# Four held first-layer tiles in two PSUM banks instead of three in three

## The chip, the cores and the metric

The kernel runs on one core of one Trainium2 chip. The metric is the time of one execution on the device in microseconds (us); a kernel is judged by the median of its runs. Beside the timed runs one execution was taken by the hardware profiler; all rows below are from it. Engines are PE (matmuls), PEld (its weight loads), ACT, DVE and POOL; SP issues the DMA loads and stores.

## The reference

Three layers follow each other, all in fp32. 1152 tokens (2 batches of 576) have width 512, in attention 8 heads of 64.

```python
# 1. attention: a coarse part on means of 4 positions, and a local part
a = softmax(scale * q_d @ k_d.T) @ v_d            # repeated 4 times along the sequence
l = softmax(where(abs(i - j) < 4, scale * q @ k.T, -1e9)) @ v
x = repeat(a, 4) + l                              # 1152 x 512
# 2. a feed-forward layer
h = x @ w_in                                      # 512 -> 2048
x = (h / (1 + exp(-h))) @ w_out                   # 2048 -> 512
# 3. four experts, each weighted by p
y = sum(p[:, e:e+1] * (relu(x @ w1[e]) @ w2[e]))  # 512 -> 1024 -> 512
```

## The kernel before

Each fp32 product is made of three matmuls on rounded operands (high x high, high x low, low x high), so an operand is kept as a high part (`xh`, `gh`) and a low part (`xl`, `gl`). Tokens are worked on in chunks of 256, 320, 256 and 320 columns.

**Attention** is cut into 16 jobs (batch, half of the sequence, pair of heads), numbered 0 to 15; jobs 0 to 3 give the four 128-row slices (`hp`) of x for chunk 0, jobs 4 to 7 those for chunk 1, and so on. Of a job: scores on PE (L328, L334), maximum and subtraction on DVE (L341, L342), exponentials on ACT (L346, L368), the coarse scores (L352), sums and normalisation on DVE (L349, L366 to L377), transposes on PE (L388, L390) that ACT evacuates (L391 to L398), products with the values (L416, L420), and the split into `xh` (ACT, L432) and `xl` (DVE, L433).

**The feed-forward layer** takes its weights in units of 2048 columns; units 0 and 1 are for the first layer of the first half (8 tiles of 128 features), units 2 and 3 for its second layer, unit 4 is the first of the second half. Each unit is loaded in four quarters of 512 KB (L164) into one of three staging tiles. A quarter is rebuilt from a packed form: two passes on ACT (L189, L190), two on DVE (L191, L195; the second frees the staging tile, and with it the next load), then ACT rounds the high part (L197) and POOL subtracts to get the low part (L198). The first layer of a tile (`g1_step`) is 12 matmuls into a PSUM bank of the pool `mm`, which has three; its evacuation (`g1_evac`) is a tanh on ACT (L514), a product on DVE (L515), and one step later the split into `gh` (L520) and `gl` (L521). The second layer (`g2_step`) adds up 24 matmuls per tile over the 8 feature tiles.

**The hold.** While attention for chunk 0 runs, the first tiles of its first layer are already summed up, slice by slice as the jobs deliver it (`start_mm`, one call per `hp`). They stay in their banks until the main loop reaches them and only evacuates them.

**The order.** Every step has a priority (`prio`, ticks in `at_tick`); a scheduler lays the instructions of each engine into a fixed list from these and from its own estimate of the durations, so a different hold changes the lists of all engines as far as they are not tied. On the chip each engine works its list strictly in order, SP too: an instruction that waits holds up all behind it.

Of the kernel before, what the change touches and what calls it, by code (L numbers as in the profile page):

```python
# [21 lines left out]
HP = NH // 2  # L22
# [18 lines left out]

SPLIT_AT = (-14, -11, -8, -6, -4, -4, -4, -4, -1, -1)
LOAD_AT = (-27, -13, -10)
HOLD = 3
LEAD_LOAD = 23
LEAD_SPLIT = 8
LEAD_ATTN = 11
# [14 lines left out]
def attention_moe_kernel(ctx, tc, kqa, kqb, qtl, va, vb, w64, w1d, w2d, dpr, out):  # L62
    nc = tc.nc
    PE, ACT, DVE, POOL, SP = nc.tensor, nc.scalar, nc.vector, nc.gpsimd, nc.sync
# [57 lines left out]
    def follow(i, earlier, reason):  # L122
        tc.add_manual_dep(i.ins, earlier.ins.name, mybir.DependencyInfo(mybir.DependencyClass.NoSync, mybir.DependencyReason.DATA),
                          reason=reason)
# [192 lines left out]
    def after(i, earlier):  # L317
        follow(i, earlier, "PSUM bank")
# [174 lines left out]
    def mm3(ps, pairs, first, last):  # L493
        n = len(pairs)
        ins = [PE.matmul(out=ps, lhsT=l, rhs=r, start=(first and i == 0), stop=(last and i == n - 1))  # L495
               for i, (l, r) in enumerate(pairs)]
        return ins[0], ins[-1]

    def g1_pairs(u0, ft, k, c):
        wh, wl = unit[u0 + ft // 4]  # L500
        s = slice(k * 512 + (ft % 4) * 128, k * 512 + (ft % 4) * 128 + 128)
        return [(wh[:, s], xh[:, k, c]), (wh[:, s], xl[:, k, c]), (wl[:, s], xh[:, k, c])]
# [8 lines left out]
    def g1_evac(ps, ft, n):  # L511
        th = tmp_p[0].tile([128, tmp_p[1]], F32, tag="th", name="th")
        gf = tmp_p[0].tile([128, tmp_p[1]], F32, tag="gf", name="gf")
        ACT.activation(out=th[:, 0:n], in_=ps[:, 0:n], func=ACTF.Tanh, scale=0.5)  # L514
        DVE.scalar_tensor_tensor(out=gf[:, 0:n], in0=th[:, 0:n], scalar=1.0, in1=ps[:, 0:n],  # L515
                                 op0=ALU.add, op1=ALU.mult)
        flush()

        def fin():
            latest[ACT] = ACT.activation(out=gh[ft][:, 0:n], in_=gf[:, 0:n], func=ACTF.Copy)  # L520
            latest[DVE] = DVE.tensor_tensor(out=gl[ft][:, 0:n], in0=gf[:, 0:n], in1=gh[ft][:, 0:n].bitcast(F32), op=ALU.subtract)  # L521

        pend.append(fin)

    def mm_tile():
        return mm_p.tile([128, 512], F32, tag="mm", name="mm")
# [239 lines left out]
    hold = []  # L766

    def start_mm(hp):
        for i in range(HOLD):
            if hp == 0:  # L770
                hold.append(mm_tile())
            mm3(hold[i][:, 0:256], g1_pairs(0, i, hp, slice(0, 256)), hp == 0, hp == HP - 1)

    main_parts.append(start_mm)
    plan_jobs()
    for hp in range(HP):
        at_tick(FIRST + PER * hp + 8, 9, start_mm, hp)
# [31 lines left out]
    def next_step(n=1):  # L809
        prio(step[0])  # L810
        step[0] += n

    for hf in range(2):
        u0 = 4 * hf
        dt = 48 / (12 * len(CHUNKS[hf]))
        for ci, (o, n) in enumerate(CHUNKS[hf]):
            lastc = ci == len(CHUNKS[hf]) - 1
            for ft in range(8):
                next_step(dt)
                if hf == 0 and ci == 0 and ft < HOLD:  # L820
                    g1_evac(hold[ft], ft, 256)
# [138 lines left out]
```

## Time and profile before

| | |
|---|---|
| median of 3 runs | 691.39 us |
| lowest and highest | 689.97 and 691.98 us |
| span of the profiled execution, first to last instruction | 693.6 us |
| mean granted TensorE clock in it | 0.974 |
| PE / DVE / ACT / POOL busy | 659.5 / 440.3 / 332.0 / 247.5 us |

Of the profiled execution only the span is given, no time of its own. A row of the timeline reads: start in us, duration in us, engine, line, operation, tile written <- tiles read, number of instructions, and in brackets the idle time of the engine just before and what ended it. Durations of matmuls contain their way through the array, so that neighbours overlap.

### The profile page before, as it was taken

Reading aid. Unit: us, or ns where it says so; the run is one execution under the profiler, and the core shown is the slowest. Engines: PE = TensorE matmul, PEld = TensorE weight load, DVE = VectorE, ACT = ScalarE, POOL = GpSimd, SP = SyncE. Lnnn points to the kernel's source line nnn. Section 1 sums busy time; section 2 is a strip of 40 time slices with the busy share of each in tenths; the row PEclk is TensorE's granted clock in tenths of the full one; section 3 lists DMA queues with packets and bytes.
Section 4 is the critical chain, followed back from the end, with each engine's and each line's share of the span. In section 5 each row is a group of like instructions: output and inputs, shape, how many; then the busy total and the mean of one; then the engine's idle time right before and its main releaser. Section 6 shows DMA issues by size and latency. Waiting matters only on the chain.

```text
span 693.6 us, 13797 instructions
## 1 busy us (share of the span) xinstructions
PE 659.5 (95%) x5516; PEld 641.9 (93%) x5516; DVE 440.3 (63%) x882; ACT 332.0 (48%) x753; POOL 247.5 (36%) x346
## 2 busy tenths in 40 slices
PE   4779779999999999999999999999999999999996
PEld 3659669999999999999999999999999999999996
DVE  4678967638664643675665985548855669756444
ACT  4559766647653532544335643345533356433321
POOL 4344762114240000344264432456232654322210
PEclk9597989999999999999999999999999999999999
DMA  8665663105250210042001420004300010000001
GB/s 248 215 183 166 184 176 96 34 1 161 92 174 1 81 44 1 1 144 70 1 1 48 136 61 1 1 2 122 93 31 1 1 60 3 1 32 17 17 31 45
DMA packets 16927, 48.16 MB, mean 69 GB/s; under 512 B 2976, under 2 KB 4256, under 8 KB 16864
## 3 DMA queue, kind: packets, MB, share of 16 engines
q1 hardware_dynamic: 16864, 47.29, 22.0%
q8 instruction: 43, 0.70, 0.4%
q14 instruction: 20, 0.16, 0.1%
HBM read 44.93 MB, written 2.36 MB: 68 GB/s over the span
## 4 chain that ended last, share of the span: by engine, by line
PE 83%; DMA 6%; DVE 6%; ACT 2%; issue 2%; POOL 1%; SPq 0%; ACTq 0%; DVEq 0%; POOLq 0%
PE mm L495 53%; PE p L699 26%; DMA stg<-in_w_dram 3%; DMA vg<-in_va_dram 2%; DVE dec L191 1%; DVE dec L195 1%; DVE gl L521 1%; PE s L328 1%; PE o L420 1%; PE t L388 1%; PE o L416 1%; DVE acc L727 1%; DVE gf L515 0%; POOL vg L265 0%; PE s L352 0%
## 5 line engine op out<-in xcount | busy, mean ns | idle before, releaser
L495 PE MATMUL mm<-xh,wbuf 128*128 128x256 f32 (+2 forms) x1280 | 268.7, 296 | 3.4 <-ACT xh L432 2.6
L495 PEld LDWEIGHTS mm<-xh,wbuf 128*128 128x128 f32 x1280 | 211.0, 190 | 4.7 <-ACT xh L432 3.0
L495 PE MATMUL mm<-xl,wbuf 128*128 128x256 f32 (+2 forms) x640 | 189.8, 297 | 0.0
L681 POOL TENSOR_TENSOR r<-r 128x128 f32<-128x128 f32 x160 | 93.5, 597 | 183.2 <-ACT r L675 143.7
L684 DVE TENSOR_TENSOR h<-r,h 128x384 fp32r<-128x384 f32 (+1 forms) x128 | 91.4, 717 | 64.6 <-ACT h L683 64.4
L495 PEld LDWEIGHTS mm<-xl,wbuf 128*128 128x128 f32 x640 | 121.6, 190 | 0.1
L683 ACT ACTIVATE h<-r 128x384 fp32r<-128x384 f32 (+1 forms) x128 | 73.2, 577 | 85.3 <-POOL r L681 54.1
L495 PE MATMUL mm<-gh,wbuf 128*128 128x256 f32 (+2 forms) x512 | 106.0, 300 | 6.4 <-ACT wbuf L197 3.5
L699 PE MATMUL p<-wext,h 128*128 128x256 f32 x672 | 91.5, 279 | 0.0
L495 PEld LDWEIGHTS mm<-gh,wbuf 128*128 128x128 f32 x512 | 83.8, 191 | 8.0 <-ACT wbuf L197 3.7
L699 PE MATMUL p<-wbuf,h 128*128 128x256 f32 x672 | 84.5, 278 | 0.0
L699 PEld LDWEIGHTS p<-wext,h 128*128 128x128 f32 x672 | 84.4, 188 | 0.0
L699 PEld LDWEIGHTS p<-wbuf,h 128*128 128x128 f32 x672 | 81.2, 188 | 0.0
L495 PE MATMUL mm<-gl,wbuf 128*128 128x256 f32 (+2 forms) x256 | 74.7, 296 | 0.5 <-DVE gl L521 0.5
L675 ACT ACTIVATE r<-mm 128x512 f32<-128x512 f32 x48 | 28.7, 597 | 75.5 <-PE mm L495 75.1
L681 DVE TENSOR_TENSOR r<-r 128x128 f32<-128x128 f32 x96 | 33.5, 349 | 37.7 <-ACT r L675 33.0
L495 PEld LDWEIGHTS mm<-gl,wbuf 128*128 128x128 f32 x256 | 48.6, 190 | 0.8 <-DVE gl L521 0.8
L521 DVE TENSOR_TENSOR gl<-gf,gh 128x256 fp32r<-128x256 f32 (+2 forms) x64 | 34.8, 547 | 18.0 <-ACT gh L520 15.4
L198 POOL TENSOR_TENSOR wbuf<-dec,wbuf 128x512 fp32r<-128x512 f32 x24 | 32.5, 1360 | 31.1 <-ACT wbuf L197 20.2
L727 DVE SCALAR_TENSOR_TENSOR acc<-p,pr,acc 128x256 f32<-128x256 f32 (+1 forms) x63 | 36.1, 605 | 5.9 <-PE p L699 5.9
L626 POOL TENSOR_TENSOR wext<-kst,wext 128x512 fp32r<-128x512 f32 x8 | 10.7, 1344 | 78.4 <-ACT wext L624 42.9
L515 DVE SCALAR_TENSOR_TENSOR gf<-th,mm 128x256 f32<-128x256 f32 (+2 forms) x64 | 28.4, 449 | 15.3 <-ACT th L514 13.6
(122 smaller groups left out, 980.2 us busy)
## 6 DMA issues: line engine op xcount, KB each, us to landing
stg<-in_w_dram SPq DMA_DIRECT2D x32, 512.0 KB, 4.3
kst<-in_w2d_dram SPq DMA_DIRECT2D x16, 512.0 KB, 3.6
kst<-in_w1d_dram SPq DMA_DIRECT2D x12, 512.0 KB, 3.6
kq<-in_kqa_dram SPq DMA_DIRECT2D x8, 419.0 KB, 3.3
kq<-in_kqb_dram SPq DMA_DIRECT2D x8, 323.0 KB, 10.8
vg<-in_va_dram SPq DMA_DIRECT2D x8, 288.0 KB
stg<-in_w1d_dram SPq DMA_DIRECT2D x4, 512.0 KB
vw<-in_vb_dram SPq DMA_DIRECT2D x8, 180.0 KB
```

Source lines behind the costliest of these rows:

```text
L191: i = DVE.scalar_tensor_tensor(out=ai, in0=ai, scalar=3, in1=v[:, :, 0], op0=ALU.logical_shift_left, op1=ALU.bitwise_or)
L198: POOL.tensor_tensor(out=l[:, c], in0=a, in1=h[:, c].bitcast(F32), op=ALU.subtract)
L495: ins = [PE.matmul(out=ps, lhsT=l, rhs=r, start=(first and i == 0), stop=(last and i == n - 1)) for i, (l, r) in enumerate(pairs)]
L515: DVE.scalar_tensor_tensor(out=gf[:, 0:n], in0=th[:, 0:n], scalar=1.0, in1=ps[:, 0:n], op0=ALU.add, op1=ALU.mult)
L521: latest[DVE] = DVE.tensor_tensor(out=gl[ft][:, 0:n], in0=gf[:, 0:n], in1=gh[ft][:, 0:n].bitcast(F32), op=ALU.subtract)
L626: b = eng.tensor_tensor(out=l[:, r], in0=x, in1=h[:, r].bitcast(F32), op=ALU.subtract)
L675: ACT.activation(out=r[:, 0:4].rearrange("p s t -> p (s t)"), in_=ps[:, 0:512], func=ACTF.Relu)
L681: latest[eng] = eng.tensor_tensor(out=r[:, o], in0=r[:, a], in1=r[:, b], op=op)
L683: ACT.activation(out=h, in_=r[:, part], func=ACTF.Copy)
L684: latest[DVE] = DVE.tensor_tensor(out=l, in0=r[:, part], in1=h.bitcast(F32), op=ALU.subtract)
L699: ins = [PE.matmul(out=ps, lhsT=x, rhs=y, start=(opens and k == 0 and i == 0), stop=(k == 3 and i == n - 1), skip_group_check=True) for i, ...
L727: DVE.scalar_tensor_tensor(out=o, in0=ps, scalar=p, in1=o, op0=ALU.mult, op1=ALU.add)
```

## The change

`HOLD` goes from 3 to 4, and a held tile is 256 columns wide, half a bank, so two tiles share one. Only the first matmul of the bank opens it (`start`); the first of the second tile is put behind that one. The third bank of `mm` is free during the hold.

```diff
-HOLD = 3
+HOLD = 4
...
     def start_mm(hp):
         for i in range(HOLD):
-            if hp == 0:
-                hold.append(mm_tile())
-            mm3(hold[i][:, 0:256], g1_pairs(0, i, hp, slice(0, 256)), hp == 0, hp == HP - 1)
+            if hp == 0 and i % 2 == 0:
+                t = mm_tile()
+                hold.extend([t[:, 0:256], t[:, 256:512]])
+            pairs = g1_pairs(0, i, hp, slice(0, 256))
+            for m, (l, r) in enumerate(pairs):
+                opens = hp == 0 and m == 0
+                p = PE.matmul(out=hold[i], lhsT=l, rhs=r, start=opens and i % 2 == 0,
+                              stop=(hp == HP - 1 and m == len(pairs) - 1), skip_group_check=True)
+                if opens and i % 2 == 0:
+                    opened = p
+                elif opens:
+                    after(p, opened)
```

The lists of the engines change with it. PE, at the end of the hold: the last slice of the held tiles and what follows. Before (`mm_338`, `mm_342`, `mm_346` are the three held tiles, `mm_791` the next tile, `s_708` the scores of job 6):

```order
L495 MATMUL mm_338<-xl_94,wbuf_97 128x256
L495 MATMUL mm_338<-xh_93,wbuf_97 128x256
L495 MATMUL mm_342<-xl_94,wbuf_97 128x256
L495 MATMUL mm_342<-xh_93,wbuf_97 128x256
L495 MATMUL mm_346<-xl_94,wbuf_97 128x256
L495 MATMUL mm_346<-xh_93,wbuf_97 128x256
L328 MATMUL s_708<-kq_519 64x70 x10
L334 LDWEIGHTS ident16_119
L334 MATMUL s_708<-mask_120,ident16_119 128x350
L495 MATMUL mm_791<-xh_93,wbuf_97 128x256
```

And of the change (`mm_338` and `mm_345` hold two tiles each, `mm_858` is the fifth tile, `s_719` job 6's scores):

```order
L495 MATMUL mm_858<-xh_93,wbuf_97 128x256 x2
L495 MATMUL mm_858<-xl_94,wbuf_97 128x256
L776 MATMUL mm_338<-xl_94,wbuf_97 128x256
L776 MATMUL mm_338<-xh_93,wbuf_97 128x256 x2
L776 MATMUL mm_338<-xl_94,wbuf_97 128x256
L776 MATMUL mm_338<-xh_93,wbuf_97 128x256
L776 MATMUL mm_345<-xl_94,wbuf_97 128x256
L776 MATMUL mm_345<-xh_93,wbuf_97 128x256 x2
L776 MATMUL mm_345<-xl_94,wbuf_97 128x256
L776 MATMUL mm_345<-xh_93,wbuf_97 128x256
L495 MATMUL mm_858<-xh_93,wbuf_97 128x256
L328 MATMUL s_719<-kq_524 64x70 x10
```

Four tiles are finished there in place of three, and matmuls of a fifth stand between them, ahead of job 6's scores.

SP, where the loads of the last quarters of unit 3 and the first of unit 4 go out. Before (`stg64_789` is quarter 3 of unit 3, `stg64_858` and `stg64_891` quarters 0 and 1 of unit 4, `kq_1076` and `kq_1226` are K and Q of jobs 10 and 11, `vg` value groups, `vw` value windows):

```order
L164 DMA stg64_789<-in_w64_dram 128x512
L244 DMA kq_1076<-in_kqa_dram 128x838
L257 DMA vg_1288<-in_va_dram 72x1024
L164 DMA stg64_858<-in_w64_dram 128x512
L250 DMA vw_1027<-in_va_dram 72x512
L164 DMA stg64_891<-in_w64_dram 128x512
L244 DMA kq_1226<-in_kqa_dram 128x838
```

And of the change (`stg64_800`, `stg64_856`, `stg64_889` are the same three quarters, `kq_1074` and `kq_1224` the same K and Q; `vg_1413` is that of job 11):

```order
L164 DMA stg64_800<-in_w64_dram 128x512
L250 DMA vw_1025<-in_va_dram 72x512
L164 DMA stg64_856<-in_w64_dram 128x512
L244 DMA kq_1074<-in_kqa_dram 128x838
L257 DMA vg_1413<-in_va_dram 72x1024
L250 DMA vw_1178<-in_va_dram 72x512
L244 DMA kq_1224<-in_kqa_dram 128x838
L164 DMA stg64_889<-in_w64_dram 128x512
```

Quarter 0 of unit 4 moves ahead of job 10's K and Q; quarter 1 moves behind job 11's.

ACT at the same place. Before (`dec_884` is quarter 2 of unit 3 on its way, `dec_933` quarter 3):

```order
L189 ACTIVATE dec_933<-stg64_789 128x512
L190 ACTIVATE stg64_858<-stg64_858 128x512
L432 ACTIVATE xh_93<-o_961 128x320
L197 ACTIVATE wbuf_97<-dec_884 128x512
L398 ACTIVATE atd0_1218<-t2_1209 72x256
L197 ACTIVATE wbuf_97<-dec_933 128x512
L368 ACTIVATE ed_1221,st_1137<-s_1127,st_1137 128x144
L190 ACTIVATE stg64_891<-stg64_891 128x512
```

And of the change (`dec_882` is quarter 2 of unit 3, `dec_931` quarter 3):

```order
L190 ACTIVATE stg64_856<-stg64_856 128x512
L423 ACTIVATE od_1117<-o_1102 128x80
L197 ACTIVATE wbuf_97<-dec_882 128x512
L378 ACTIVATE ed_1069<-ed_1069,st_992 128x144
L432 ACTIVATE xh_93<-o_1102 128x320
L189 ACTIVATE dec_931<-stg64_800 128x512
L368 ACTIVATE ed_1219,st_1135<-s_1125,st_1135 128x144
L391 ACTIVATE at_1208<-t1_1206 70x512
L398 ACTIVATE atd0_1216<-t2_1207 72x256
L189 ACTIVATE dec_2156<-stg64_856 128x512
L190 ACTIVATE stg64_889<-stg64_889 128x512
L197 ACTIVATE wbuf_97<-dec_931 128x512
```

In both, the first pass over quarter 0 of unit 4 stands ahead of the rounding of quarter 2 of unit 3. The first pass over quarter 1 of unit 4 stood behind the rounding of quarter 3 of unit 3 and now stands ahead of it.

## Rows read from the trace of the kernel before

**Rows 1.** The page, busy time of PE, share of the span, instructions.

```profile
PE 659.5 (95%) x5516; PEld 641.9 (93%) x5516; DVE 440.3 (63%) x882; ACT 332.0 (48%) x753; POOL 247.5 (36%) x346
```

**Rows 2.** Busy time by stretch, with granted clock, DMA share, GB/s at the end.

```profile
60.00:93.00 33.00, 24.30 (x293) 21.41 (x291) 26.61 (x59) 23.76 (x62) 19.66 (x24) 1.00 0.60 182
82.00:92.00 10.00, 6.26 (x76) 5.03 (x74) 5.52 (x15) 5.09 (x14) 6.66 (x9) 1.00 0.89 268
93.00:105.00 12.00, 11.95 (x119) 10.79 (x120) 9.34 (x21) 8.40 (x22) 10.21 (x14) 0.72 0.54 153
...
140.00:200.00 60.00, 58.65 (x474) 56.89 (x473) 38.56 (x64) 39.36 (x86) 19.36 (x14) 1.00 0.32 104
200.00:300.00 100.00, 100.00 (x768) 99.81 (x767) 52.19 (x104) 42.99 (x96) 14.40 (x14) 1.00 0.13 40
```

**Rows 3.** PE in order of time, from the second layer to chunk 1.

```profile
68.92 0.28 PE L495 MATMUL mm<-gh,wbuf 128*128 128x256 f32 x1
...
93.05 0.38 PE L495 MATMUL mm<-gh,wbuf 128*128 128x256 f32 x1 [3.53 <-ACT wbuf L197]
...
95.57 0.80 PE L495 MATMUL mm<-gh,wbuf 128*128 128x256 f32 x2
...
105.11 0.30 PE L495 MATMUL mm<-xh,wbuf 128*128 128x320 f32 x1
...
107.54 0.46 PE L416 MATMUL o<-atd,vd 72*64 72x64 f32 x8
107.82 0.64 PE L420 MATMUL o<-at,vw 70*64 70x64 f32 x16
```

**Rows 4.** ACT in order of time: tanhs, then passes over weight quarters.

```profile
55.55 0.66 ACT L514 ACTIVATE th<-mm 128x256 f32<-128x256 f32 x2
...
69.33 0.68 ACT L189 ACTIVATE dec<-stg 128x512 f32<-128x512 f32 x1
...
91.50 0.65 ACT L190 ACTIVATE stg<-stg 128x512 int32<-128x512 uint16 x1 [3.78 <-DMA stg<-in_w_dram]
...
92.38 0.62 ACT L197 ACTIVATE wbuf<-dec 128x512 fp32r<-128x512 f32 x1
...
93.64 0.63 ACT L197 ACTIVATE wbuf<-dec 128x512 fp32r<-128x512 f32 x1 [0.37 <-DVE dec L195]
```

**Rows 5.** DVE in order of time, 62 to 88 us.

```profile
62.72 0.53 DVE L341 TENSOR_REDUCE st<-s 128x5 f32<-128x350 f32 x1 [1.35 <-PE s L334]
...
81.48 1.13 DVE L195 SCALAR_TENSOR_TENSOR dec<-stg,dec 128x512 int32<-128x512 int32 x1
82.53 0.43 DVE L341 TENSOR_REDUCE st<-s 128x4 f32<-128x280 f32 x1
...
86.93 0.67 DVE L195 SCALAR_TENSOR_TENSOR dec<-stg,dec 128x512 int32<-128x512 int32 x1
```

**Rows 6.** SP's DMA issues in order of time.

```profile
60.30 0.33 SPq L164 DMA_DIRECT2D stg<-in_w_dram  x1
...
81.03 0.33 SPq L244 DMA_DIRECT2D kq<-in_kqa_dram  x1
81.46 0.34 SPq L257 DMA_DIRECT2D vg<-in_va_dram  x1
82.68 0.34 SPq L164 DMA_DIRECT2D stg<-in_w_dram  x1
...
88.04 0.43 SPq L244 DMA_DIRECT2D kq<-in_kqa_dram  x1
```

**Rows 7.** DMA issues of 55 to 100 us: count, KB each, median us to landing.

```profile
stg<-in_w_dram SPq DMA_DIRECT2D x9, 512.0 KB, 5.1
vg<-in_va_dram SPq DMA_DIRECT2D x3, 288.0 KB
kq<-in_kqa_dram SPq DMA_DIRECT2D x2, 419.0 KB
```

**Rows 8.** POOL in order of time, at 81 us.

```profile
81.40 1.50 POOL L265 TENSOR_TENSOR kq<-kq 128x288 f32<-128x288 f32 x2 [0.79 <-PE s L328]
```

## The prediction

> **What bounds the kernel now.** I read the page first: PE is busy for 659.5 us of a 693.6 us span, so 34 us of it are idle [rows 1]. Next the busy time by stage, to see where these lie. From 200 to 300 us PE is busy throughout, from 140 to 200 for 58.65 of 60 us; but 60 to 93 us holds 33.00 - 24.30 = 8.7 us without PE work, and from 93 to 105 us the granted clock is 0.72 on average, between TensorE's levels of 2.4 GHz (1.00) and 1.2 GHz (0.50), right after PE's longest wait [rows 2]. So the change can count almost only through the moment at which the first matmul of chunk 1 (320 columns wide) starts, 105.11 us [rows 3], and through attention work that is done ahead of it. From there all that follows moves as one block.
>
> What sets that moment is read from PE's instructions in order of time: its longest wait, 3.53 us, is ended at 93.05 by ACT's L197, the rounding of a weight piece [rows 3]. I call the pieces u.j (unit, quarter); this one is 3.2. Followed back on ACT, L197 of 3.2 at 92.38 had nothing of its own to wait for: DVE's L195 had finished that piece at 86.93 + 0.67 = 87.60 [rows 4, 5]. It stood behind ACT's L190 of piece 4.0, which waited 3.78 us for its load [rows 4]. That load went out at 82.68, when L195 of piece 3.1 freed the staging tile (81.48 + 1.13), and was there at 91.50: 8.8 us [rows 4 to 6]. The median of this line from 55 to 100 us is 5.1 [rows 7]. In front of it on SP were K/Q of job 10 (419 KB, 81.03) and the same job's value groups (288 KB, 81.46), and the DMA engines moved 268 GB/s, 0.89 busy, from 82 to 92 us [rows 2, 6, 7].
>
> **The change part by part.** The profiled span, 693.6, is 2.2 us above the median of the three timed runs, 691.39. No row says why; I work out a shift on the span's rows and put it on the median unchanged.
>
> *The fourth held tile.* 12 matmuls move from behind the hold into it. Dense first- and second-layer matmuls take 100 us for 768, 0.13 each [rows 2], so this is 1.6 us, double at the half clock. They, and the first matmuls of the fifth tile in the bank that is now free, run earlier; but PE idles 8.7 us between 60 and 93, waiting for weights that do not depend on it, so on its own this is worth nothing: the next wait starts earlier and ends when it did.
>
> *Two tiles in one bank.* ACT's tanh of tile 1 now waits for DVE's L515 of tile 0. Before, the two tanhs, on two banks, run together in 0.66 us at 55.55 [rows 4]. The serial chain adds one L515 per pair of tiles, a DVE pass over 256 columns like L341's over 280, 0.43 us [rows 5]. Nobody reads these tiles before the second layer starts at 68.92 [rows 3], 13 us later; without that cover it would cost 0.9 for two pairs. The Trainium skill (PSUM — Partial Sum Buffer, "PSUM bank collisions raise a hardware error") says why the wait is there: two engines may not touch one bank in the same partitions at once, two readers included. No run here shows a collision, and by that rule the sum stays as it is.
>
> *DVE's list up to piece 3.1.* Attention runs further ahead: job 9's L341 and L342 and job 5's L433 now stand before L195 of piece 3.1, three instructions of about 0.43 us [rows 5], 1.3 us. In exchange job 7's scores come soon behind job 6's on PE, so that the 1.35 us for which DVE waited for them, before 62.72, should go [rows 5]. I take 0. The bounds are wider: DVE instructions are drawn out beside POOL's (L195 took 1.13 us at 81.48 and 0.67 at 86.93, the first beside POOL's L265 [rows 5, 8]), POOL's now fall beside others, about 0.5 us each time, and job 10's value groups go out ahead of piece 3.2's load (288 KB, 1.1 us at 268 GB/s). I allow 2 us either way.
>
> *Load of piece 2.3.* It moves behind two K/Q loads and job 6's values on SP, from 60.30 [rows 6] to about 64, when PE should be through job 4's values. With 5.1 us it lands at 69.1; ACT's L189 of that piece, the pass that DVE waits for, came only at 69.33 [rows 4]. That hides it, just; each us more would be a us on the chain.
>
> *Load of piece 4.0, ahead of the 707 KB.* It still goes out when L195 of 3.1 ends, 82.7, with 5.1 us now [rows 7]: ACT's L190 starts at 87.8 and L197 of 3.2 ends at 87.8 + 0.65 + 0.62 = 89.0, not 93.0 [rows 4]. PE's wait of 3.53 us goes. Bounds: 8.8 us again (no gain), or so early that L195 of 3.2 at 87.60 decides (88.2).
>
> *What is late next.* ACT's new order has L190 of piece 4.1 ahead of L197 of piece 3.3. Behind that L190 stand L197 of 3.3, job 10's exponentials and job 8's evacuations, and PE waits for all of them. The load of 4.1 needs 3.2's staging tile (87.60) and now stands behind K/Q of job 11, which went out at 88.04 [rows 6]: issued 88.1, landed 93.2 with 5.1 us. L190 (0.65) and L197 (0.63) then end at 94.5, against 94.3 before [rows 4]. Piece 3.3 comes as before, then, but PE meets it with less left to do. Before, PE took the first matmul of 3.3 at about 95.8 [rows 3]: matmuls of 3.2 and job 7's values filled 93.05 to 95.6. Gain 95.8 - 94.5 = 1.3. Three more matmuls of 3.2 are also done, 0.26 each at the half clock: 0.8. And job 9's values, which stood behind chunk 1's start (107.54 to 108.46 [rows 3]), are done before it: 0.9. Sum 3.0 us. I leave the half clock as it is, since PE still has a wait of some us in front of the same work.
>
> A rule of the Trainium skill bears on the load of 4.1 (DMA: Bandwidth & Descriptors, "Queues, rings and completion order"): loads of one issuing queue are taken in ring order on each DMA engine. The 8.8 us of piece 4.0 behind 707 KB agree. By ring order 4.1 comes after 4.0, job 10's K/Q, job 11's value groups and K/Q and a small load, over 1638 KB, and with its own 512 KB that is 8.0 us at 268 GB/s [rows 2]; from 82.7, with 3.2 us of latency (an estimate: 5.1 less 512 KB at that rate), it would land at 93.9 and the sum would be 2.3. This neither turns the sign nor leaves the range.
>
> **Rivals.**
> - *No second wait.* If 4.1 lands by 91.5, 3.3 is ready when PE gets to it and PE runs through from 89.0: 93.0 - 89.0 = 4.0, plus 0.9 for job 9's values, 686.5. If the clock then also stays at 1.00 where it was 0.72 for 12 us, 0.28 x 12 = 3.4 us more: 683.1. For it: DVE and ACT reach attention earlier, so 3.2 may leave DVE before 87.6. Against: 268 GB/s at 0.89 busy is about what the DMA engines give here.
> - *The wait moves and grows (slower).* The load of 4.1 takes the 8.8 us that 4.0 took: issued 88.1, landed 96.9, L197 of 3.3 ends at 98.2, PE is 2.4 behind at that point, less 0.8 and 0.9: 0.7 later; with DVE's 1.3 us uncovered as well 2.0, 693.4. It decides from a landing at 96.2. For it: four loads in front where 4.0 had two. Against: the first of them go out 5 us ahead of 4.1.
> - *DVE's list is the pace.* The attention work ahead of 3.0 and 3.1 is not covered, POOL takes another part, and the gain is eaten: 690 to 692. For it: DVE is busy for 26.61 of the 33 us from 60 to 93 [rows 2]. That the change does nothing, because the same waits end last, looks the same.
>
> **How the numbers follow.** Forecast 0.45, at 691.4 - 3.0 = 688.4; no second wait 0.20; slower 0.15; DVE's pace 0.20. About 0.3%, 2.1 us, is what a measurement can tell from no change. Of the forecast's 0.45, 0.32 lie beyond that (a landing of 4.1 up to 0.9 us later), 0.12 within, 0.01 slower; no second wait is all faster; of the slower rival 0.13 count as slower, the rest within; of DVE's pace 0.19 are within, 0.01 slower. Faster 0.52, same 0.33, slower 0.15. The range leaves out the far end of the second case and the slowest tenth: 684.5 to 693.0. The forecast's own, from DVE's 2 us either way, is 686.4 to 690.4.
>
> **What would show it.** Right: ACT's L190 of piece 4.0 without a wait of over 2 us, and L197 of 3.2 before 90; then a wait of PE ended by L197 of 3.3, itself behind L190 of 4.1; chunk 1's first matmul at about 103 with job 9's values ahead of it; 200 us onward unchanged but for the shift. Wrong: piece 3.1 leaving DVE more than 2 us later than 82.6, a landing of 4.1 after 96, or new waits of PE after 105.

## The result and the profile after

The change is slower: 695.22 us median (692.19 to 700.33, 18 runs) against 690.06 (686.51 to 694.18, 18 runs), ratio 1.008 [1.0063, 1.0096], 5.2 us. The profiled execution of it has a span of 698.5 us and a time of 700.33, 5 us over its median. In all executions whose span and time are both known, the time is 1.8 to 2.3 us above the span; for before it is 2.0 to 2.3. So the profiled execution of before, with its span of 693.6, took some 695.7: above all 18 of its runs, and some 5.6 us over their median, where the prediction set only the span beside a median and got 2.2. Both first traces show untypical executions; a second was taken of each.

The page of the change, the row that answers to [rows 1]:

```profile
PE 658.2 (94%) x5516; PEld 639.6 (92%) x5516; DVE 444.5 (64%) x882; ACT 331.9 (48%) x753; POOL 248.8 (36%) x346
```

PE does the same work and idles 6 us longer. Where, the busy times by stretch tell (as in [rows 2]: PE, PEld, DVE, ACT, POOL, then the granted clock, DMA share, GB/s). The change:

```profile
50.00:60.00 10.00, 5.46 (x49) 4.64 (x49) 4.18 (x12) 4.60 (x14) 1.39 (x2) 0.67 0.62 207
60.00:93.00 33.00, 25.89 (x298) 21.70 (x294) 29.88 (x64) 26.17 (x69) 23.91 (x29) 0.95 0.65 189
93.00:105.00 12.00, 8.49 (x89) 7.04 (x90) 10.86 (x20) 6.54 (x17) 7.99 (x11) 0.84 0.58 164
...
200.00:300.00 100.00, 99.73 (x784) 98.93 (x782) 55.28 (x107) 46.59 (x103) 14.11 (x13) 1.00 0.15 48
```

And before, in a stretch that [rows 2] leave out:

```profile
50.00:60.00 10.00, 8.70 (x58) 7.61 (x59) 8.92 (x23) 8.63 (x24) 4.57 (x6) 0.50 0.66 218
```

Between 50 and 60 us PE, DVE and ACT work about half of the time, where before they worked for over 8 of the 10 us, and POOL hardly does. From 200 to 300 us nothing that counts differs. I follow that stall back. PE in the change, in order of time:

```profile
48.86 0.51 PE L352 MATMUL s<-kd,qbd 128*128 128x144 f32 x2 [1.64 <-POOL qbd L265]
...
54.42 0.28 PE L495 MATMUL mm<-xh,wbuf 128*128 128x256 f32 x1
58.81 1.43 PE L328 MATMUL s<-kq 64*64 64x70 f32 x20 [4.12 <-ACT ed L368]
```

In before the same scores of job 6 start 3.9 us earlier:

```profile
54.93 1.43 PE L328 MATMUL s<-kq 64*64 64x70 f32 x20 [0.60 <-ACT ed L368]
```

The exponentials L368 that PE waits for stand on ACT behind L190 of piece 1.3, which waits for its load. ACT in the change:

```profile
50.23 0.66 ACT L189 ACTIVATE dec<-stg 128x512 f32<-128x512 f32 x1
56.29 0.65 ACT L190 ACTIVATE stg<-stg 128x512 int32<-128x512 uint16 x1 [5.40 <-DMA stg<-in_w_dram]
...
58.29 0.38 ACT L368 ACTIVATE ed<-s,st 128x144 f32<-128x144 f32 x1
```

ACT before:

```profile
51.73 0.68 ACT L190 ACTIVATE stg<-stg 128x512 int32<-128x512 uint16 x1 [0.55 <-DMA stg<-in_w_dram]
...
54.42 0.36 ACT L368 ACTIVATE ed<-s,st 128x144 f32<-128x144 f32 x1
```

The load's issue on SP, in the change (K and Q of job 7, the value windows of job 5, then 1.3 as the first of two L164):

```profile
48.83 0.35 SPq L244 DMA_DIRECT2D kq<-in_kqb_dram  x1
49.28 0.34 SPq L252 DMA_DIRECT2D vw<-in_vb_dram  x1
49.72 0.82 SPq L164 DMA_DIRECT2D stg<-in_w_dram  x2
```

And before:

```profile
43.91 0.35 SPq L244 DMA_DIRECT2D kq<-in_kqb_dram  x1
45.78 0.30 SPq L252 DMA_DIRECT2D vw<-in_vb_dram  x1
47.81 0.97 SPq L164 DMA_DIRECT2D stg<-in_w_dram  x2
```

Job 7's K/Q go out 4.9 us later, and 1.3, which stands behind them, 1.9 later. From its issue to ACT's L190 it then takes 56.29 - 49.72 = 6.6 us instead of 3.9, with K/Q and windows (323 and 180 KB) issued right in front of it. The Trainium skill (DMA: Bandwidth & Descriptors, "Queues, rings and completion order") has the descriptors of one queue taken in ring order on each DMA engine; that agrees: 503 KB at the 268 GB/s of [rows 2] are 1.9 us (an estimate), of the 2.7 that the flight grew.

What K/Q of job 7 waited for, SP's waits from 30 to 66 us tell (in total, times, longest):

```profile
SPq L244 <- POOL qbd L265: 8.0, 4, 5.1
```

The longest was 1.5 us before. `qbd` are sums over job 5's Q, read from the buffer that the load of job 7's K and Q needs. On POOL stands the cause. In the change:

```profile
41.82 0.65 POOL L265 TENSOR_TENSOR qbd<-kq 64x64 f32<-64x64 f32 x2
45.60 1.29 POOL L265 TENSOR_TENSOR vg<-vg 72x512 f32<-72x512 f32 x1 [3.13 <-DMA vg<-in_va_dram]
46.85 0.88 POOL L265 TENSOR_TENSOR kq<-kq 128x128 f32<-128x128 f32 x1
47.81 0.99 POOL L265 TENSOR_TENSOR qbd<-kq 64x64 f32<-64x64 f32 x2
```

And before:

```profile
42.71 0.42 POOL L265 TENSOR_TENSOR kq<-kq 128x128 f32<-128x128 f32 x1
43.21 0.67 POOL L265 TENSOR_TENSOR qbd<-kq 64x64 f32<-64x64 f32 x2
45.72 1.49 POOL L265 TENSOR_TENSOR vg<-vg 72x512 f32<-72x512 f32 x1 [1.83 <-DMA vg<-in_va_dram]
```

It is the first row in which POOL's two lists differ at all (`-` before, `+` the change; `vg` is the fold of job 8's value groups, `kq` and `qbd_122` job 5's sums):

```order
 L265 TENSOR_TENSOR qbd_121<-kq 64x64 x2
+L265 TENSOR_TENSOR vg<-vg 72x256x2
 L265 TENSOR_TENSOR kq<-kq 128x64x2
 L265 TENSOR_TENSOR qbd_122<-kq 64x64 x2
-L265 TENSOR_TENSOR vg<-vg 72x256x2
```

The fold waits for a load that lands at 45.6, whichever way round. Behind it before stood nothing urgent; now job 5's sums do. So one moved row on POOL goes through SP's list to ACT's list to PE: 3.9 us of stall, 35 us ahead of the wait that the prediction worked on. There the steps come as forecast but late. The change's DVE (L195 of piece 3.1) and ACT (L190 of 4.0, L197 of 3.2, L190 of 4.1, L197 of 3.3), answering to [rows 4, 5]:

```profile
85.97 1.08 DVE L195 SCALAR_TENSOR_TENSOR dec<-stg,dec 128x512 int32<-128x512 int32 x1
...
91.60 0.67 ACT L190 ACTIVATE stg<-stg 128x512 int32<-128x512 uint16 x1 [0.82 <-DMA stg<-in_w_dram]
...
93.32 0.63 ACT L197 ACTIVATE wbuf<-dec 128x512 fp32r<-128x512 f32 x1 [0.94 <-DVE dec L195]
...
98.91 0.69 ACT L190 ACTIVATE stg<-stg 128x512 int32<-128x512 uint16 x1
99.49 0.62 ACT L197 ACTIVATE wbuf<-dec 128x512 fp32r<-128x512 f32 x1
```

Piece 3.1 leaves DVE at 87.05 and not 82.61 [rows 5], 4.4 us late, the stall and half a us. L190 of 4.0 starts 4.5 us after its load went out at 87.11, no longer 8.8. PE, answering to [rows 3]:

```profile
94.18 0.99 PE L388 MATMUL t<-ident,sm 128*70 128x128 f32 x4 [2.11 <-DVE sm L377]
...
100.17 0.38 PE L495 MATMUL mm<-gh,wbuf 128*128 128x256 f32 x1 [0.30 <-ACT wbuf L197]
...
103.17 0.60 PE L388 MATMUL t<-ident,sm 128*70 128x128 f32 x4 [2.03 <-DVE sm L377]
...
112.36 0.30 PE L495 MATMUL mm<-xh,wbuf 128*128 128x320 f32 x1
```

The 3.53 us wait for piece 3.2 is gone, the wait for 3.3 is 0.30, but DVE's normalisation (L377) holds PE twice for 2 us, and chunk 1 starts 7.25 us later than in the first trace of before. Each time L377 stands on DVE behind weight passes that are drawn out, while POOL works beside them, to 1.75 and 2.17 us (L191) and in between 2.40 (L195, at 97.05):

```profile
90.81 1.75 DVE L191 SCALAR_TENSOR_TENSOR dec<-dec,stg 128x512 int32<-128x512 int32 x1
...
100.49 2.17 DVE L191 SCALAR_TENSOR_TENSOR dec<-dec,stg 128x512 int32<-128x512 int32 x1
```

### The profile page after: what moved, and what is told of

Its sections match the earlier page's. It is cut to its first block, busy times and chain, and to the rows that moved or that the text cites. A ratio compares the mean times of both kernels' runs of the same rounds, so it can differ in the third digit from the quotient of the medians.

```text
span 698.5 us, 13793 instructions
## 1 busy us (share of the span) xinstructions
PE 658.2 (94%) x5516; PEld 639.6 (92%) x5516; DVE 444.5 (64%) x882; ACT 331.9 (48%) x753; POOL 248.8 (36%) x346
## 4 chain that ended last, share of the span: by engine, by line
PE 83%; DVE 7%; DMA 5%; ACT 2%; issue 1%; POOL 1%; SPq 1%; ACTq 0%; POOLq 0%
PE mm L495 52%; PE p L699 25%; DMA stg<-in_w_dram 4%; DVE dec L191 2%; PE s L328 1%; DVE dec L195 1%; DVE gl L521 1%; PE t L388 1%; PE o L420 1%; DMA vg<-in_va_dram 1%; PE o L416 1%; DVE st L373 1%; DVE acc L727 1%; ACT dec L189 0%; PE s L352 0%
## 5 line engine op out<-in xcount | busy, mean ns | idle before, releaser
L495 PE MATMUL mm<-xh,wbuf 128*128 128x256 f32 (+2 forms) x1248 | 260.8, 296 | 2.1 <-DVE st L367 1.1
L495 PEld LDWEIGHTS mm<-xh,wbuf 128*128 128x128 f32 x1248 | 204.2, 188 | 3.2 <-DVE gf L515 2.9
L495 PE MATMUL mm<-xl,wbuf 128*128 128x256 f32 (+2 forms) x624 | 183.6, 294 | 0.0
L495 PEld LDWEIGHTS mm<-xl,wbuf 128*128 128x128 f32 x624 | 117.6, 188 | 0.0
L198 POOL TENSOR_TENSOR wbuf<-dec,wbuf 128x512 fp32r<-128x512 f32 x24 | 32.5, 1363 | 27.3 <-ACT wbuf L197 15.8
L515 DVE SCALAR_TENSOR_TENSOR gf<-th,mm 128x256 f32<-128x256 f32 (+2 forms) x64 | 28.4, 448 | 18.7 <-ACT th L514 17.8
```

The source lines that it names most:

```text
L198: POOL.tensor_tensor(out=l[:, c], in0=a, in1=h[:, c].bitcast(F32), op=ALU.subtract)
```

## The experiments

All ratios are to before on the same chip, with 95% intervals; "us" is the median. The first theory is the fold on POOL, told above (each of the texts below counts its theories anew). Its rivals: the shared bank, the held tile, DVE's list.

**The row on POOL alone, taken back and put in.** The change with the fold behind job 5's sums; no other row of any list moves:

```diff
...
-            fold(j.vg)
+            i = fold(j.vg); j.i == 8 and follow(i, last_kq[5], "K and Q first")
...
```

> The changed kernel with one row of one list moved: on POOL the fold of job 8's value groups stands behind the sums of job 5's K and Q again, as in the kernel before. All other lists are those of the change. Theory 1 (a queue at 45 us): in the trace of the change that fold waits for its load until 45.60 and so holds up job 5's sums, the next K/Q load on SP (48.83 for 43.91), the load of piece 1.3 behind it, ACT's L190 of that piece (waits 5.40 us) and PE (4.12 us before job 6's scores). Then PE's wait falls to under 1 us, job 6's scores start near 55, chunk 1 near 108.4 instead of 112.36, and the time is about 4 us below the change's: 691 against the kernel before at 690. Theory 2 (two tiles in a bank cost the time, by the serial tanh and DVE reads or by waits in the bank): the wait at 55 may go but the kernel stays within 1 us of the change's 695. Theory 3 (the waits behind 90 us take up what is saved, since they have other causes): chunk 1 starts at 111 to 112 all the same, 694 to 695.

Before with the fold ahead of them:

```diff
...
-            fold(j.vg)
+            i = fold(j.vg); j.i == 8 and follow(first_kq[5], i, "value groups first")
...
```

> The kernel before with the same single row moved the other way: on POOL the fold of job 8's value groups ahead of the sums of job 5's K and Q. Three held tiles in three banks, all other lists as before. Theory 1: the chain of waits of the change appears in it too: POOL held until about 45.6, the load of piece 1.3 landing near 56, a wait of PE of about 4 us before job 6's scores, and 3 to 4 us more: 693 to 694. Theory 2 (the two tiles in a bank cost the time): within 1 us of the kernel before. Theory 3 (the later waits of weights take up the delay, since PE idles 8.7 us between 60 and 93 anyway): a wait near 55, but chunk 1 within 1 us of 105.1 and the time within 1 us.

Measured: the first 691.91 us, 1.0039 [1.0014, 1.0064]; the second 693.09, 1.0054 [1.0029, 1.0078]. The row alone makes before slower by 0.54%, with the same chain. ACT and PE of the second:

```profile
55.36 0.65 ACT L190 ACTIVATE stg<-stg 128x512 int32<-128x512 uint16 x1 [4.10 <-DMA stg<-in_w_dram]
...
58.52 1.43 PE L328 MATMUL s<-kq 64*64 64x70 f32 x20 [4.11 <-ACT ed L368]
```

But taking it back returns only half of the 0.8%. PE of the first kernel has no stall, and chunk 1 at 104.24, but two waits that [rows 3] do not show:

```profile
54.91 0.83 PE L328 MATMUL s<-kq 64*64 64x70 f32 x20 [0.96 <-ACT ed L368]
...
67.31 0.39 PE L495 MATMUL mm<-xh,wbuf 128*128 128x256 f32 x1 [1.57 <-DVE st L367]
...
72.84 0.39 PE L495 MATMUL mm<-gh,wbuf 128*128 128x256 f32 x1 [1.96 <-DVE gf L515]
```

Only the wait of 1.57 is new. The second stands in before too:

```profile
71.67 0.38 PE L495 MATMUL mm<-gh,wbuf 128*128 128x256 f32 x1 [1.90 <-DVE gf L515]
```

**The held tile and the bank.** The change's code with three tiles, and before with two:

```diff
-HOLD = 4
+HOLD = 3
```

> The code of the change with three held tiles in place of four (two in one bank, the third alone in the second). Its POOL list has job 8's fold ahead of job 5's sums as in the change, though no fourth tile is held. Theory 1 (the order of the lists sets the time, the fourth tile nothing): the stall at 54 to 59 us is there, and the time is 693 to 697, like the change's. Theory 2 (the fourth tile costs it): 690 to 691.

```diff
-HOLD = 3
+HOLD = 2
```

> The kernel before with two held tiles in place of three, each in its own bank; its SP and POOL lists are those of the kernel before. If a held tile is worth nothing by itself, since PE waits for weights between 60 and 93 us whatever it has done ahead, the time is within 1 us of the kernel before (690). If each held tile is worth its 12 matmuls (1.6 us, twice that at the lower clock), it is 1.6 to 3.2 us slower.

The second edit tests nothing. The third tile's matmuls, no longer held, are laid in the same places, and the program is that of before: the same instructions in the same order on all five engines, with the same operands and waits. Its 689.13, 0.9997 [0.9971, 1.0022], is before measured once more, and its trace is one more of before. Three tiles in the change's code come to 696.63, 1.0118 [1.0081, 1.0154], but the scheduler laid the lists anew there, with the fold ahead again (PE's stall 3.32 us) and another wait of 3.91 at 71, so that run does not price the bank. A kernel that changes a size here can change the lists too, so from here on they were tied.

**Code and lists apart.** Each instruction of ACT, DVE, POOL and SP is tied behind the one that precedes it in a table; PE stays free. The code, with the table of one kernel's lists put on the other's code:

```diff
+    finish(*before, tick_of(NE, 0, 0) + 2); pin(engines, follow)
...
+    for eng, order in zip(engines, ORDER):
+        for x, y in zip(order, order[1:]):
+            follow(eng.made[y], eng.made[x], "order")
```

The change with before's four lists, before with the change's, the change itself once more, and the change with only SP's and POOL's lists of before:

> The changed kernel (four held tiles, two to a bank), with the lists of ACT, DVE, POOL and SP tied, instruction by instruction, to those of the kernel before; only PE's list is free. It splits the cost of the change, 5.2 us, into code and lists. Theory 1 (the lists cost it: the row on POOL at 45 us about 3 us, as its two tests showed, and further rows behind 60 us the rest): within 1 us of the kernel before. Theory 2 (two tiles in a bank cost what is left when the row on POOL is moved back, 2.7 us): 2 to 3 us slower than before.

> The counterpart: the kernel before (three held tiles, three banks) with the lists of ACT, DVE, POOL and SP tied to those of the change; only PE's list is free. Theory 1 (the lists cost it): 4 to 6 us slower than before, a ratio near 1.007, with the wait of 4 us before job 6's scores. Theory 2 (the code costs 2.7 us, the row on POOL the rest): 3 us slower, near 1.004. The three tiles held alone might also make the new lists worse, as three packed tiles did (1.0118): then over 1.009, and the fourth tile is worth something where the lists are bad.

> The changed kernel itself once more, for a second trace beside kernels on the same chip: its profiled execution was 5 us above the median of its runs, the slowest of 18. All theories: a ratio of 1.006 to 1.010 again. Theory 1: PE's wait before job 6's scores is 3.5 to 4.5 us again, since the order causes it, and not a slow load of that one execution. What differs between the two traces behind 60 us (two waits of 2 us on DVE, the clock of 0.73 from 100 to 110 us) is that one execution's, not the change's.

> The changed kernel with the lists of SP and POOL alone tied to those of the kernel before; ACT, DVE and PE are laid out around them. Theory 1a (what is left of the cost behind the row on POOL comes with the order of loads and POOL's sums): within 1 us of the kernel before. Theory 1b (it comes with ACT's and DVE's order, the attention moved ahead of weight pieces): 2 to 3 us slower, as with the one row alone. Theory 2 (two tiles in a bank): 2 to 3 us slower too; the first of these runs tells the two apart.

Then before's code with the change's lists but the fold back in its place (49; 22 to 24 are job 5's sums), and three tiles in the change's form on before's lists:

```diff
-    [... 10,11,49,22,23,24,18,19 ...]   # POOL
+    [... 10,11,22,23,24,49,18,19 ...]
```

> The kernel before (three tiles, three banks) with the lists of the change, but the fold of job 8 behind job 5's sums: the cell that is missing beside 1.0084 (all lists of the change), 1.0054 (the fold alone) and 1.0039 (the same lists under the changed code). If the fold is all that the lists cost: 1.000 to 1.002. If the rows behind 60 us cost the rest: 1.003 to 1.005, and the code nothing.

> Three held tiles, two of them in one bank, under the lists of the kernel before. With four tiles in two banks these lists gave 1.0027. If two tiles in a bank cost about 2 us by the bank that comes free only when both are read (waits of PE for L515 near 55 and 65 us): 1.002 to 1.003 again. If the fourth tile's 12 matmuls ahead of job 6's scores cost it: 1.000 to 1.001.

Measured, as ratio to before:

| code | lists of before | and fold ahead | the change's, fold back | the change's |
|---|---|---|---|---|
| before | 1 | 1.0054 [1.0029, 1.0078] | 1.0048 [1.0024, 1.0072] | 1.0084 [1.0050, 1.0117] |
| change | 1.0027 [1.0005, 1.0049] | | 1.0039 [1.0014, 1.0064] | 1.0082 [1.0051, 1.0112] |

With SP's and POOL's lists alone the change has 1.0021 [0.9997, 1.0045]; three packed tiles on the old lists 1.0007 [0.9983, 1.0032]. In the second trace of the change (span 692.5) the stall is there again, 2.70 us, but not DVE's two waits of 2 us (0.49 now), and chunk 1 starts at 106.25. Under its own lists the code of the change costs nothing that shows (the two right columns agree up and down), and before's code is as slow with them. Half of the cost is the fold, half the other rows. The three packed tiles say that two tiles in a bank are hidden; whether the fourth on the old lists costs something (1.0027 against 1.0007, with intervals that overlap) is not settled.

**The place that the prediction worked on.** Before profiled again; before with 4.0 ahead of job 10's loads on SP (38 is 4.0, 45 and 49 the K/Q and value groups); before with L190 of 4.0 (236) behind L197 of 3.2 and 3.3 (108, 117) on ACT:

```diff
-    [... 39,37,45,49,38,44,40 ...]   # SP
+    [... 39,37,38,45,49,44,40 ...]
...
-    [... 115,236,124,108,140,117,141 ...]   # ACT
+    [... 115,124,108,140,117,236,141 ...]
```

> The kernel before itself, for a second trace. In the first, PE's longest wait behind 60 us was 3.53 us, ended by the rounding of piece 3.2, behind a load of piece 4.0 that took 8.8 us. In the traces of four other kernels with the same rows there, this wait was 0.8, 1.3, 1.5 and 2.7 us. Theory A (the profiled execution was a slow one, and the prediction took its wait for the rule): the wait is 1 to 2.5 us here, and the span 686 to 690 against 693.6. Theory B (3.5 us is the rule for this kernel): 3 to 4 us again, span near 693.

> The kernel before with one row of SP moved, all other lists tied as they were: the load of piece 4.0 goes out ahead of K/Q and value groups of job 10 (707 KB). It is the step from which the prediction took its gain, alone. By the prediction's sum the load lands after 5.1 us in place of 8.8, ACT's L190 of 4.0 no longer waits and PE's wait for piece 3.2 goes: 3 us faster or more (ratio 0.995). Theory A (that wait is 1 to 1.5 us in most executions): about 1 us faster, 0.998 to 0.999. Rival (the 707 KB come later in exchange, and job 10's attention ends the next wait): no change or slower, 1.000 to 1.002, with new waits of PE for job 10's scores behind 95 us.

> The kernel before with one row of ACT moved, all other lists tied as they were: the first pass over piece 4.0 (L190), which waits for its load, stands behind the rounding of pieces 3.2 and 3.3 (L197) in place of ahead of it. It takes away the same wait as the run before, without moving a transfer. If PE's wait for piece 3.2 sets the start of chunk 1: PE takes 3.2 near 89 by the first trace, 3.5 us earlier at most and 1 to 1.5 us in a usual execution, so 1 to 2 us faster (0.997 to 0.9985). If other waits take its place: 0.999 to 1.001.

The second trace of before (span 690.1) has no wait for piece 3.2. ACT's L190 of 4.0 there, and chunk 1:

```profile
88.32 0.67 ACT L190 ACTIVATE stg<-stg 128x512 int32<-128x512 uint16 x1 [0.63 <-DMA stg<-in_w_dram]
...
100.69 0.30 PE L495 MATMUL mm<-xh,wbuf 128*128 128x320 f32 x1
```

The load took 82.07 to 88.32, 6.2 us and not 8.8. Over seven traces with before's order here the wait for 3.2 was 3.53, 0 and 2.7 in the three of before's program, and 0.8, 1.3, 1.3 and 1.5 in the others. Both ways of removing it bring nothing that shows: 690.58, 1.0010 [0.9982, 1.0038], and 690.02, 1.0011 [0.9982, 1.0040]. In the first PE then waits 1.10 for POOL's L198 of the same piece at 92.02; in the second L197 of 3.3 waits 2.58 for DVE.

**The way from POOL to PE.** The change with only the load of 1.3 (24) put ahead of job 7's K/Q and job 5's windows (29, 28) on SP; POOL stays as it is:

```diff
-    [... 23,22,29,28,24,25,26 ...]   # SP
+    [... 23,22,24,29,28,25,26 ...]
```

> The changed kernel with one row of SP moved, all other lists as in the change: the load of piece 1.3 goes out ahead of job 7's K/Q and windows. POOL still folds job 8's value groups ahead of job 5's sums. If the cost of that fold goes through SP's queue (piece 1.3 stuck behind a K/Q load that waits for job 5's sums, then sharing the DMA engines with it), PE's wait before job 6's scores falls from 2.7 to 4.1 us to under 1 us and the time falls as it did when the fold itself was moved back: about 2.8 us under the change, a ratio near 1.004. If it goes through PE's coarse scores, which wait 1.6 us for the late sums, most of it stays: 1.006 to 1.008.

693.68, 1.0041 [1.0011, 1.0070]: as much comes back as from the fold itself. ACT's L190 of 1.3 in it no longer waits, though POOL's fold does, for 3.12 us:

```profile
50.32 0.68 ACT L190 ACTIVATE stg<-stg 128x512 int32<-128x512 uint16 x1
```

The price is paid on SP's list, where a weight load stands behind a load that waits for its buffer.

**The other half.** All with the fold back. First the load of 4.1 (40) ahead of job 11's K/Q (48) on SP, and L197 of 3.3 (117) ahead of L190 of 4.1 (239) on ACT; then DVE's L515 of the fifth tile (120) ahead of attention; POOL's sums of job 8 (40 to 32) ahead of job 9's (44, 46); and the last two together:

```diff
-    [... 47,48,40 ...]   # SP      [... 239,117 ...]   # ACT
+    [... 47,40,48 ...]             [... 117,239 ...]
...
-    [... 111,90,84,105,127,120,106 ...]   # DVE
+    [... 111,120,90,84,105,127,106 ...]
...
-    [... 41,44,46,40,42,43,32,64 ...]   # POOL
+    [... 41,40,42,43,32,44,46,64 ...]
```

> The changed kernel with the fold of job 8 moved back behind job 5's sums (as in the first run), and besides the load of piece 4.1 ahead of job 11's K/Q on SP and the rounding of piece 3.3 ahead of the first pass over 4.1 on ACT. Those two rows are the prediction's step on what is late next. With the fold alone moved back the kernel was at 1.0039, its counterpart over SP at 1.0041, and in the latter's trace PE waited 2.95 us for piece 3.3 behind piece 4.1. If that wait is what is left of the cost: 1.001 to 1.002. If what is left lies in the attention that was moved ahead, or in the code: 1.003 to 1.005 again.

> The changed kernel with job 8's fold moved back (1.0039 in the first run), and on DVE the evacuation of the fifth tile (L515) ahead of job 4's addition (L425), a weight pass (L195) and two maxima (L366), behind which it stood. In the trace of the first run PE waited 1.57 us for the bank of that tile, at 67.31. If that wait is part of what is left (2.7 us): 1.5 us less, 1.0015 to 1.0025. If the wait comes back later (PE waits for the second layer's first evacuation anyway, 1.96 us at 72.84): 1.0035 to 1.0045. PE's list, which is free, also changes a little behind 90 us.

> The changed kernel with job 8's value fold moved back, and on POOL the fold of job 9's K/Q behind job 8's sums and the piece that follows them. In the trace of the first run POOL folds the K/Q of both jobs back to back (3.41 us), and PE waits 1.03 us for job 8's sums and 0.83 us for the piece (84 to 86 us). If these are part of what is left: up to 1.9 us less, 1.001 to 1.002. If job 9's sums, which come later, take it back: 1.0035 to 1.0045.

> Both of these rows. If the rest of the cost is these two waits, 0.9995 to 1.001. If it is spread over the attention that DVE and POOL do ahead of weight pieces, so that another wait stands behind each, 1.003 or more.

1.0040 [1.0020, 1.0061], 1.0054 [1.0027, 1.0081], 1.0033 [1.0008, 1.0058] and 1.0043 [1.0016, 1.0071]: none returns it. The second case was read from DVE's list in before's code with the change's lists and the fold back, where L515 frees the bank that PE waits for:

```profile
63.43 0.48 DVE L425 TENSOR_TENSOR o<-o,od 128x320 f32<-128x320 f32 x1
63.83 1.44 DVE L195 SCALAR_TENSOR_TENSOR dec<-stg,dec 128x512 int32<-128x512 int32 x1
65.20 0.51 DVE L366 TENSOR_REDUCE st<-s 128x1 f32<-128x144 f32 x2
65.63 0.40 DVE L515 SCALAR_TENSOR_TENSOR gf<-th,mm 128x256 f32<-128x256 f32 x1
...
66.09 0.38 PE L495 MATMUL mm<-xh,wbuf 128*128 128x256 f32 x1 [1.08 <-DVE st L367]
```

(The wait is put down to L367, but the matmul needs the bank, so L515 is my reading.) With L515 first that wait falls to 0.32; the wait of 1.9 to 2.1 of the other traces is then 2.63, at 72.29, and one of 2.25 follows at 83.91, behind an L191 that took 4.88 us on DVE. No version beat before.

Seventeen of the traces, cut at two rows of PE, show where each half lies (lowest to highest, us; in brackets how many traces, those with one more row moved among them; the right column is the rest of the span; the other three have lists of none of these rows):

| lists | start to job 6's scores | to chunk 1 | to the end |
|---|---|---|---|
| before's (7) | 52.6 to 54.9, and 58.3 | 44.7 to 50.2 | 585.8 to 589.4 |
| before's, fold ahead (1) | 58.5 | 44.6 | 587.4 |
| the change's, fold back (6) | 52.0 to 54.9 | 49.3 to 54.4 | 585.4 to 589.0 |
| the change's (3) | 56.9 to 58.8 | 49.4 to 53.6 | 585.8 to 586.3 |

The 58.3 is the run with two held tiles, which is before's program. It is late without the stall: POOL waits 4.17 us for the load `qt` there, for 2.17 in the first trace, and PE 2.87 for `qbd` at 45.33. So one trace's first column alone does not tell the fold; the stall does, PE's wait for L368 ahead of job 6's scores, 2.70 to 4.49 us in the four traces with the fold ahead and at most 1.02 in the other thirteen. The other rows act in the second column: means of 46.9 us with before's lists and 51.4 with the change's and the fold back, with 0.4 less from chunk 1 on. That agrees with 0.4 to 0.5% each. Which rows of the second stretch do it is open. DVE is busy there for 40.5 to 42.6 us in the eight traces of the two upper rows and for 41.8 to 48.6 in the nine of the two lower ones (means 41.4 and 44.4): with the change's lists more of DVE's work, or longer passes, lies ahead of chunk 1. That fits, but no run shows that it is the cause.

## Why the prediction was wrong

It forecast 688.4, in a range of 684.5 to 693.0, with 0.15 for slower; measured are 695.22. The sign and the range are wrong.

- *The count of what is moved* is the first step that failed. The parts follow the lists from SP's load of 2.3 at 60.30 on; of anything earlier only the tiles themselves have a part, and "The fourth held tile" put that at nothing, since the next wait "starts earlier and ends when it did". POOL's list had changed 15 us before that, and its row was in no term. It costs 0.54% alone, about 3.7 us.
- *"Load of piece 4.0"* holds in its mechanism. In the change with the fold back, ACT's L190 of 4.0 follows its issue at 82.87 within 4.3 us and waits for nothing, and L197 of 3.2 ends at 90.4 (forecast 89.0):

```profile
87.12 0.68 ACT L190 ACTIVATE stg<-stg 128x512 int32<-128x512 uint16 x1
...
89.73 0.63 ACT L197 ACTIVATE wbuf<-dec 128x512 fp32r<-128x512 f32 x1 [0.54 <-DVE dec L195]
```

- *The sum of 3.0 us* is the second: its main term was a wait of 3.53 us that is 0 in the second trace of before and 2.7 in the third, and that brings nothing that shows when it is taken away alone in either of two ways (1.0010 and 1.0011). From the forecast to the measured time it is 8.2 us against before: roughly 3.0 for this gain, 2.8 for the fold (by taking it back) and 2.7 for the other rows.
- *"DVE's list up to piece 3.1"*, 0 with 2 us either way: 3.1 left DVE at 82.81 with the fold back, against 82.61 [rows 5], as predicted; the extra attention work shows elsewhere, as waits of PE for L515, L367 and L377 in many small parts; that these make up the second half is argued and not shown. In its mechanism that half is nearest to the rival "DVE's list is the pace", but that rival put 690 to 692 beside 691.4, no change, and the change with the fold back is 0.39% slower.
- *The fourth held tile*, worth nothing, is not shown: no run holds one tile less and differs in that alone, apart from the pair of 1.0027 and 1.0007 on before's lists, which does not settle it. *Two tiles in one bank*, hidden: borne out by three packed tiles on the old lists. Under before's lists the second tanh of a pair waits 0.49 us for L515. The Trainium skill's rule that two engines may not access one bank in the same partitions at the same time (PSUM — Partial Sum Buffer, "PSUM bank collisions raise a hardware error") fits that; no run shows a collision.
- *Load of piece 2.3*: issued at 67.41 and not at 64, the stall's 4 us; with the fold back 63.19.
- *The wait moves and grows* is seen at 2.95 us for L197 behind L190 of 4.1 with the load of 1.3 first, and at 1.42 in before's code with the change's lists and the fold back; in both traces of the change it is 0.3 or nothing.
- *Job 9's values* do come before chunk 1, from 106.42 on, and 200 us onward is unchanged. Of the signs that I named for "wrong", the first came true: 3.1 left DVE 4.4 us later than 82.6. So did the second, a landing of 4.1 after 96: its load went out at 93.35, last of those in flight, and the DMA engines still moved 225 GB/s from 96.5 to 97. They gave 381 GB/s in the half us before, so the 268 of [rows 2] is not what they give at most, as one rival had it.

## What to carry to other kernels

Where a size changes what a scheduler lays, compare every engine's whole list, the queues and POOL too, from the first row that differs, and look first for a row that waits for a DMA and has moved ahead of one that frees a buffer. Before a gain is sized by one wait, see that wait in a second execution. See also that an edit shows in the lists at all: holding two tiles left the program as it was. A stall of the whole machine is paid nearly in full, while a single wait in a stage where several engines are close to the pace gives nothing back; tying the lists shows which of the two a change touches.

## What was not expected of the hardware

- The same load of 512 KB, in the same place of SP's list behind the same 707 KB, took 8.8, 6.2 and 8.0 us in three executions of before's program (from its issue at 82.68, 82.07 and 84.85 to ACT's L190).
- DVE's two passes over a weight piece (L191, L195) take 0.64 to 0.70 us each where POOL does nothing beside them, 191 passes from 30 to 125 us in all traces. All 139 that took over 0.9 had POOL at work beside them; the longest took 4.88, with the fifth tile's L515 put first:

```profile
77.23 4.88 DVE L191 SCALAR_TENSOR_TENSOR dec<-dec,stg 128x512 int32<-128x512 int32 x1
```

- The granted clock from 0 to 30 us is 0.76 in the first trace of before and in both of the change, and 1.00 (2.4 GHz, the upper of its two levels, throughout) in the second trace of before and in the change with the fold back. PE is busy for 16.8 to 18.5 us of it in all five, and the rows show no reason; this stretch took no longer at 0.76: SP's next K/Q load (L244) went out at 29.8 to 30.6 us in the three, at 30.1 and 30.8 in the two.
